# Packed values made in transposed form, and three first halves that share the first layer

## The chip, the cores and the metric

One Trainium2 chip, one core of it. The metric is the device time of one execution in microseconds. Of the kernel before, three runs were timed: 1183.54 us in the median, 1183.08 to 1184.45. TensorE (PE) multiplies, with its weight loads as a row of their own (PEld); VectorE is DVE, ScalarE is ACT, GpSimd is POOL, and SP issues the DMAs.

## The reference

Packed attention followed by two dense layers, all in float32, batch 8, 8 heads, 576 rows, head size 64, 32 packed queries:

```python
p_packed = sm_attn(p, k, v)             # 32 x 64 for each batch and head
out = sm_attn(q, p_packed, p_packed)    # 576 x 64 for each batch and head
x = out.transpose(0, 2, 1, 3).reshape(4608, 512)
h = x @ w_in                            # 512 x 2048
g = where(h > 0, h, exp(min(h, 0)) - 1)
x = g @ w_out                           # 2048 x 512
h = x @ w_in2                           # 512 x 1024
solu = h * softmax(h); ln = layer_norm(solu) * g_ln
out = ln @ w_out2                       # 1024 x 512
```

The weights come as 64-bit floats and are narrowed on the chip.

## The kernel before, in words

The attention of a batch is folded into the first layer. `s1` makes the scores of the packed queries against the keys, for four heads at a time (g = 0, 1): `s1_mm` (line 228), `s1_max`, `s1_exp`, `s1_div`. The probabilities are transposed into `a_sb`, on TensorE for batches 0 and 1 (`t1_mm`, `t1_a`, lines 257 to 263), in 32x32 blocks on VectorE with moves for the later ones (`t1_blocks`, `t1_move`). `pp_mm` (lines 279 to 286) multiplies them with the values: 32 columns of probabilities are the weights, 64 columns of values move, five chunks of rows accumulate, and the four heads lie under each other in PSUM. The trace has two loads and two matmuls for each `pe.matmul` of this type, 40 of each for a run of `pp_mm`. `pp_t` (lines 288 to 295) then turns the result with eight 32x32 transposes on VectorE into `pp_t2`, which has the head's 64 columns in the partitions. `s2_mm` (line 309) makes the scores of half of a batch's 576 rows against the packed keys; `s2_tr` to `s2_split` make their softmax in blocks and split it into two parts, `AT`. `m_mm` (line 353) multiplies the packed values with a quarter c of `w_in`, and `m_a`, `m_b` split the product `M`. So the first layer of a half is `AT` times `M`.

The two layers run in steps. `steps` (lines 722 to 725) lists (batch, half, f), f being one of 16 blocks of 128 of the 2048. A step `n` does `ffn_h` (six matmuls into `h`), the items of the plan, `ffn_g` (lines 385 to 387: two ScalarE instructions and `fe` on VectorE), the split of the step before into `ghi` and `glo` (lines 394 to 396), and `ffn_x2` for the step three before (twelve matmuls with `wo[f // 2]` into `acc`). Batch 0 is done in two rounds: f = 0 to 7 for both halves (steps 0 to 15), then f = 8 to 15 (steps 16 to 31). In the first round the sum is spilled to DRAM (lines 430 to 434); `load_part` brings it back, and line 429 adds it.

Quarters c = 0, 1 of `w_in` and `w_out` blocks 0 to 3 serve the first round, the others the second. One 512-column unit of a 64-bit weight is narrowed by two ScalarE instructions (lines 112, 113), two on VectorE (114, 115) and a product on GpSimd (119); `split_w_out` then splits it on ScalarE and GpSimd.

The order comes from lists written out by hand: `put(n, ...)` attaches an item to step n; `plan_first` holds the steps to 32, `plan_attn(b)` a batch's attention in the 32 steps before its own, `plan_last` the weights of the last layers. The scheduler of the framework orders the instructions by its own model; from step 32 on TensorE alone keeps the program's order (`tc.manual_schedule`, line 739). All loads go through the one queue of SP, in order, and wait there for their buffer: the slots M0 to M4 and wo0 to wo7 hold raw weights, k, v or q before they hold their own tile. The tail (lines 742 to 772) does the two last layers in blocks of 128 rows.

Of the kernel before, what the change touches and what calls it, by code (L numbers as in the profile page):

```python
# [19 lines left out]
NP = 32  # L20
# [14 lines left out]
def attention_mlp_kernel(ctx: ExitStack, tc: tile.TileContext, q, k, v, v_tail, p,  # L35
# [139 lines left out]
    def split_w_out2(j, u):  # L175
        if u == 0:
            wo2[j] = slot(f"wo2_{j}", [P, 2, 1024], f"M{(4 * B + j) % 5}", F32R)
        cs = slice(u * DM, (u + 1) * DM)
        split(wo2[j][:, 0, cs], wo2[j][:, 1, cs], cvs.pop(("wo2", j, u)),
              scale=g_sb[:, 2 * j + u:2 * j + u + 1])  # L180
# [98 lines left out]
    def pp_mm(b, g, ps2=misc_ps):  # L279
        o = ps2(f"pp{b}_{g}")  # L280
        vv = vt.pop((b, g))
        for c in range(5):
            for h in range(4):
                pe.matmul(o[h * NP:(h + 1) * NP, 0, 0:D], a_sb[:, c, h * NP:(h + 1) * NP],
                          vv[:, c, h * D:(h + 1) * D], start=(c == 0), stop=(c == 4))
        st["pp", g] = o

    def pp_t(b, g):

        o = st.pop(("pp", g))  # L290
        for h in range(4):
            for r in range(2):
                n0 = h % 2 * 2 * NP + r * NP
                dve.transpose(pp_t2[b % 2][n0:n0 + NP, 2 * g + h // 2, :],  # L294
                              o[h * NP:(h + 1) * NP, 0, r * NP:(r + 1) * NP])
# [59 lines left out]

    def m_a(b, c):
        mt[b, c] = t = slot(f"M{b}_{c}", [P, 2, 2, 512], f"M{(4 * b + c) % 5}", F32R)
        for g in range(2):
            act.activation(t[:, 0, g], st["m"][:, g], AF.Copy, scale=WSCALE)
        m_lo(t, 0)  # L360
# [201 lines left out]
    def plan_attn(b):  # L562

        n = NSTEP * (b - 1)
        if b == 2:
            n += 2
# [7 lines left out]
        plan_m(b, 0, n + 16 + (b == 2))  # L574
        plan_s2(b, 1, n + 19 + (b == 2), (2, 4, 6, 7, 10, 11))
        plan_m(b, 1, n + 22 + (b == 2))
# [3 lines left out]
    def plan_first():  # L580
# [15 lines left out]
        put(31, (scale_g,))  # L596
# [5 lines left out]
        narrow_w_in(2, 8, 9, 10, 11)  # L602
        narrow_w_in(3, 12, 13, 14, 15)
        for j in range(4, 8):
            narrow_w_out(j, 2 * j + 8, 2 * j + 9)
        put(1, (load_w_in, 3, 0, "M3"))
        put(5, (load_w_out, 5, "M4"))
        put(9, (load_w_in, 3, 1, "wo7"))
        put(11, (load_w_out, 6, "wo6"))
        put(15, (load_w_out, 7, "wo7"))  # L610

        put(0, (s2_mm, 0, 1), (load_q, 1, 0))
        for n, item in ((0, (s2_tr, 0, 1)), (1, (s2_max, 0, 1, pool)), (2, (s2_exp, 0, 1)),
                        (3, (s2_div, 0, 1, pool)), (5, (s2_back, 0, 1)), (6, (s2_split, 0, 1, pool))):
            put(n, item)
        plan_s1(1, 0, 4)
        plan_s1(1, 1, 7)
        put(7, (load_p, 2))
        plan_pp(1, 0, 10)
        m_fast(0, 2, 14)  # L620
        m_fast(0, 3, 16)
        plan_pp(1, 1, 18)
        put(20, (load_part, 0, 0))
        put(27, (load_part, 0, 1))
        plan_s2(1, 0, 22, (1, 2, 4, 5, 7, 8))
        m_fast(1, 0, 24)
        m_fast(1, 1, 26)
        plan_s2(1, 1, 28, (1, 2, 4, 5, 7, 8))
        m_fast(1, 2, 30)
        m_fast(1, 3, 32)  # L630
# [67 lines left out]
    load_w_in(2, 0, "wo7")  # L698
# [5 lines left out]
    load_w_in(2, 1, "wo6")  # L704
# [8 lines left out]
    load_w_out(4, "wo5")  # L713
# [3 lines left out]
    for b in range(2, B):  # L717
# [3 lines left out]

    steps = [(0, half, f, f % 8 == 0, f % 8 == 7)
             for f0 in (0, 8) for half in range(2) for f in range(f0, f0 + 8)]
    steps += [(b, half, f, f == 0, f == NF - 1)
              for b in range(1, B) for half in range(2) for f in range(NF)]
# [10 lines left out]
    for n in range(NSTEP):  # L736
        step(n)

    with tc.manual_schedule(engines={mybir.EngineType.PE}):
        for n in range(NSTEP, len(steps)):  # L740
# [67 lines left out]
```

## Time and profile before

| | |
|---|---|
| median of three runs | 1183.54 us |
| the profiled execution, its own time | 1184.11 us |
| its span | 1182.3 us |
| mean granted clock of TensorE | 0.987 of full speed |
| first `h` matmul | 34.96 us |
| `fe` of step 0 ends | 43.75 us |
| `fe` of step 32 ends | 151.69 us |

The span is the time from the first to the last instruction of the one execution that the profiler recorded. Busy time counts an engine's own instructions. A wait is put down to what came last. Steps are counted by the instructions of line 387, one for each step.

### The profile page before, as it was taken

How to read it: one execution, taken by the hardware profiler on the slowest of the kernel's cores; microseconds unless marked ns; L12 is line 12 of the kernel's file. 1: busy time of each engine (PE TensorE's matmuls, PEld its weight loads, DVE VectorE, ACT ScalarE, POOL GpSimd, SP SyncE). 2: the span in 40 equal slices, each digit the busy share in tenths (PEclk: the TensorE clock that was granted, in tenths of full speed). 3: DMA queues.
4: the chain of work that ended last, by engine and by line, in shares of the span. 5: the costliest groups of instructions: out<-in, count | busy, mean ns of one | idle time of the engine just before them, and what ended most of it. 6: DMA issues, size and time to landing. Idle time of an engine off the chain costs nothing.

```text
span 1182.3 us, 20670 instructions
## 1 busy us (share of the span) xinstructions
PE 1124.3 (95%) x7916; PEld 977.2 (83%) x7916; DVE 854.4 (72%) x1928; ACT 740.5 (63%) x1587; POOL 158.6 (13%) x152
## 2 busy tenths in 40 slices
PE   5688999999999999999999989989999999999997
PEld 1477798898898898898898879978888888888886
DVE  5998876667567567566566595758878878778774
ACT  4788755655655655655655676648766766766664
POOL 2655500100100100100101130200000000000000
PEclk8899999999999999999999999999999999999999
DMA  9763322022022022022011042411111111000001
GB/s 336 295 205 118 96 63 81 21 71 90 4 74 89 3 77 87 2 79 86 1 59 44 2 148 71 143 56 54 31 51 63 34 48 63 27 19 27 28 27 36
DMA packets 39411, 86.01 MB, mean 73 GB/s; under 512 B 7440, under 2 KB 19984, under 8 KB 37392
## 3 DMA queue, kind: packets, MB, share of 16 engines
q1 hardware_dynamic: 39312, 84.69, 21.5%
q8 instruction: 62, 1.02, 0.4%
q14 instruction: 37, 0.30, 0.1%
HBM read 64.62 MB, written 20.05 MB: 72 GB/s over the span
## 4 chain that ended last, share of the span: by engine, by line
PE 46%; DVE 28%; ACT 15%; issue 7%; POOL 2%; DMA 2%; SPq 0%; POOLq 0%; ACTq 0%; DVEq 0%
PE acc L70 9%; PE acc L72 9%; PE acc L71 8%; ACT lnX L501 6%; PE h L70 5%; PE h L71 5%; PE h L72 5%; DVE lnB L491 4%; DVE ln L484 2%; PE m L303 2%; DVE z L476 2%; ACT h L479 2%; DVE a_sb L276 2%; DVE ppT L294 2%; DVE lnT L62 2%
## 5 line engine op out<-in xcount | busy, mean ns | idle before, releaser
L70 PE MATMUL acc<-ghi,wo 128*128 128x288 f32 x1024 | 308.2, 303 | 1.8 <-DVE x L433 1.0
L72 PE MATMUL acc<-glo,wo 128*128 128x288 f32 x1024 | 302.0, 296 | 2.6 <-DVE glo L396 2.5
L71 PE MATMUL acc<-ghi,wo 128*128 128x288 f32 x1024 | 302.5, 296 | 1.3 <-POOL wo L62 1.3
L70 PEld LDWEIGHTS acc<-ghi,wo 128*128 128x128 f32 x1024 | 192.5, 189 | 38.7 <-ACT fe L386 25.8
L72 PEld LDWEIGHTS acc<-glo,wo 128*128 128x128 f32 x1024 | 193.0, 189 | 4.6 <-DVE glo L396 4.6
L71 PEld LDWEIGHTS acc<-ghi,wo 128*128 128x128 f32 x1024 | 193.3, 189 | 2.8 <-POOL wo L62 2.2
L394 ACT CAST ghi<-fe 128x288 fp32r<-128x288 f32 x256 | 110.3, 432 | 132.3 <-DVE fe L387 132.0
L387 DVE SCALAR_TENSOR_TENSOR fe<-fe,h 128x288 f32<-128x288 f32 x256 | 114.9, 450 | 106.8 <-ACT fe L386 105.1
L396 DVE TENSOR_TENSOR glo<-fe,ghi 128x288 fp32r<-128x288 f32 x256 | 135.7, 531 | 76.4 <-ACT ghi L394 75.0
L518 PE MATMUL o<-wo,lnT 128*128 128x512 f32 (+1 forms) x592 | 185.5, 386 | 5.1 <-ACT lnT L61 5.1
L70 PE MATMUL h<-AT,M 128*128 128x288 f32 x512 | 155.5, 304 | 21.9 <-DVE fe L387 16.3
L385 ACT ACTIVATE fe<-h 128x288 f32<-128x288 f32 x256 | 104.4, 408 | 109.2 <-PE h L72 99.2
L501 ACT COPY lnX<-lnB 32x256 f32<-32x256 f32 x288 | 116.3, 404 | 72.8 <-DVE lnB L491 62.1
L71 PE MATMUL h<-AT,M 128*128 128x288 f32 x512 | 152.1, 297 | 0.8 <-DVE M L363 0.8
L72 PE MATMUL h<-AT,M 128*128 128x288 f32 x512 | 151.3, 296 | 0.0
L518 PEld LDWEIGHTS o<-wo,lnT 128*128 128x128 f32 x592 | 111.4, 191 | 27.7 <-ACT lnT L61 5.9
L70 PEld LDWEIGHTS h<-AT,M 128*128 128x128 f32 x512 | 96.6, 189 | 34.8 <-DVE fe L387 25.0
L386 ACT ACTIVATE fe<-fe 128x288 f32<-128x288 f32 x256 | 113.5, 444 | 6.7
L520 PE MATMUL o<-wo,lnT 128*128 128x512 f32 (+1 forms) x296 | 113.6, 385 | 0.0
L71 PE MATMUL h<-wi,x2lo 128*128 128x512 f32 x288 | 112.2, 389 | 1.1 <-DVE x2lo L62 1.1
L70 PE MATMUL h<-wi,x2hi 128*128 128x512 f32 x288 | 112.2, 389 | 0.0
L72 PE MATMUL h<-wi,x2hi 128*128 128x512 f32 x288 | 112.0, 389 | 0.0
(101 smaller groups left out, 1684.9 us busy)
## 6 DMA issues: line engine op xcount, KB each, us to landing
q<-in_q SPq DMA_DIRECT2D x16, 576.0 KB, 4.0
x_dram<-x SPq DMA_DIRECT2D x32, 288.0 KB, 2.3
x2raw<-x_dram SPq DMA_DIRECT2D x9, 1024.0 KB, 5.6
out_x<-y SPq DMA_DIRECT2D x35, 256.0 KB, 2.0
k<-in_k SPq DMA_DIRECT2D x15, 576.0 KB, 4.0
raw_wi<-in_w_in SPq DMA_DIRECT2D x8, 1024.0 KB, 9.4
v_sb<-in_v SPq DMA_DIRECT2D x15, 512.0 KB, 3.9
raw_wo<-in_w_out SPq DMA_DIRECT2D x7, 1024.0 KB, 11.6
```

The source lines that it names most:

```text
L70: pe.matmul(o, a[0], b[0], start=start, stop=False)
L71: pe.matmul(o, a[1], b[0], start=False, stop=False)
L72: pe.matmul(o, a[0], b[1], start=False, stop=stop)
L385: act.activation(e, o[:, 0:HS], AF.Relu, scale=-1.0)
L386: act.activation(e, e, AF.Exp, scale=-1.0)
L387: dve.scalar_tensor_tensor(out=e, in0=e, scalar=-1.0, in1=o[:, 0:HS], op0=ALU.add, op1=ALU.max)
L394: act.copy(ghi, e)
L396: return lambda: dve.tensor_tensor(out=glo, in0=e, in1=ghi.bitcast(F32), op=ALU.subtract)
L491: dve.transpose(t, last.pop(("ln", i)))
L501: act.copy(x, y)
L518: pe.matmul(o, t[:, x, kk], w[:, 0, cs], start=x + kk == 0, stop=x == 1 and kk == 7)
L520: pe.matmul(o, t[:, 0, kk], w[:, 1, cs], start=False, stop=False)
```

## The change

`pp_mm` takes the values as weights (64 columns) and lets the probabilities move (32 columns), so that the product comes out transposed: head 2u + r in partitions 64r to 64r + 63, columns 32u to 32u + 31. `pp_t` is one copy of 128x64. The first round of steps covers three halves, (0, 0), (0, 1) and (1, 0), with f = 0 to 7 each (steps 0 to 23), and the second round the same three with f = 8 to 15 (steps 24 to 47); the half (1, 0) is spilled and reloaded as well. The first plan is written out anew for this: the attention of batch 1 comes earlier, quarters 2 and 3 of `w_in` and blocks 4 to 7 of `w_out` later, and three weight loads leave the preamble. M slots go by a table. The scheduler orders TensorE for the first 64 steps.

```diff
@@ -174,7 +174,7 @@
 
     def split_w_out2(j, u):
         if u == 0:
-            wo2[j] = slot(f"wo2_{j}", [P, 2, 1024], f"M{(4 * B + j) % 5}", F32R)
+            wo2[j] = slot(f"wo2_{j}", [P, 2, 1024], m_slot(B, j), F32R)
         cs = slice(u * DM, (u + 1) * DM)
         split(wo2[j][:, 0, cs], wo2[j][:, 1, cs], cvs.pop(("wo2", j, u)),
               scale=g_sb[:, 2 * j + u:2 * j + u + 1])
@@ -277,22 +277,21 @@
                                 t[h * NP:(h + 1) * NP, j::4])
 
     def pp_mm(b, g, ps2=misc_ps):
+
+
         o = ps2(f"pp{b}_{g}")
         vv = vt.pop((b, g))
-        for c in range(5):
-            for h in range(4):
-                pe.matmul(o[h * NP:(h + 1) * NP, 0, 0:D], a_sb[:, c, h * NP:(h + 1) * NP],
-                          vv[:, c, h * D:(h + 1) * D], start=(c == 0), stop=(c == 4))
+        for u in range(2):
+            for c in range(5):
+                for r in range(2):
+                    h = 2 * u + r
+                    pe.matmul(o[r * D:(r + 1) * D, 0, u * NP:(u + 1) * NP], vv[:, c, h * D:(h + 1) * D],
+                              a_sb[:, c, h * NP:(h + 1) * NP], start=(c == 0), stop=(c == 4))
         st["pp", g] = o
 
     def pp_t(b, g):
-
-        o = st.pop(("pp", g))
-        for h in range(4):
-            for r in range(2):
-                n0 = h % 2 * 2 * NP + r * NP
-                dve.transpose(pp_t2[b % 2][n0:n0 + NP, 2 * g + h // 2, :],
-                              o[h * NP:(h + 1) * NP, 0, r * NP:(r + 1) * NP])
+        dve.tensor_copy(pp_t2[b % 2][:, 2 * g:2 * g + 2].rearrange("p u n -> p (u n)"),
+                        st.pop(("pp", g))[:, 0, 0:2 * NP])
 
     def packed_mm(o, b, x):
 
@@ -353,8 +352,14 @@
         packed_mm(o, b, wi[c])
         st["m"] = o
 
+    def m_slot(b, c):
+
+        k = 4 * (b - 2) + c
+        first = {(0, 0): 0, (0, 1): 1, (1, 0): 2, (1, 1): 3, (0, 2): 4, (0, 3): 0, (1, 2): 1, (1, 3): 4}
+        return f"M{first[b, c] if b < 2 else (0, 2, 3, 1, 4)[k % 5]}"
+
     def m_a(b, c):
-        mt[b, c] = t = slot(f"M{b}_{c}", [P, 2, 2, 512], f"M{(4 * b + c) % 5}", F32R)
+        mt[b, c] = t = slot(f"M{b}_{c}", [P, 2, 2, 512], m_slot(b, c), F32R)
         for g in range(2):
             act.activation(t[:, 0, g], st["m"][:, g], AF.Copy, scale=WSCALE)
         m_lo(t, 0)
@@ -562,8 +567,6 @@
     def plan_attn(b):
 
         n = NSTEP * (b - 1)
-        if b == 2:
-            n += 2
         plan_s1(b, 0, n)
         plan_s1(b, 1, n + 3)
         put(n + 3, (load_p, b + 1))
@@ -571,9 +574,9 @@
         plan_pp(b, 1, n + 10)
         plan_s2(b, 0, n + 14, (1, 2, 4, 6, 8, 9))
         n = NSTEP * (b - 1)
-        plan_m(b, 0, n + 16 + (b == 2))
-        plan_s2(b, 1, n + 19 + (b == 2), (2, 4, 6, 7, 10, 11))
-        plan_m(b, 1, n + 22 + (b == 2))
+        plan_m(b, 0, n + 16)
+        plan_s2(b, 1, n + 19, (2, 4, 6, 7, 10, 11))
+        plan_m(b, 1, n + 22)
         plan_m(b, 2, n + 25)
         plan_m(b, 3, n + 28)
 
@@ -593,41 +596,47 @@
             put(n1, (split_w_out, j, 0, pool))
             put(n1 + 1, (split_w_out, j, 1, pool))
 
-        put(31, (scale_g,))
+        put(40, (scale_g,))
         put(0, (split_w_out, 0, 0, pool), (split_w_out, 0, 1, dve))
         narrow_w_in(1, 0, 0, 1, 1)
         m_fast(0, 1, 2)
         for j in range(1, 4):
             narrow_w_out(j, 2 * j, 2 * j + 1)
-        narrow_w_in(2, 8, 9, 10, 11)
-        narrow_w_in(3, 12, 13, 14, 15)
-        for j in range(4, 8):
-            narrow_w_out(j, 2 * j + 8, 2 * j + 9)
-        put(1, (load_w_in, 3, 0, "M3"))
-        put(5, (load_w_out, 5, "M4"))
-        put(9, (load_w_in, 3, 1, "wo7"))
-        put(11, (load_w_out, 6, "wo6"))
-        put(15, (load_w_out, 7, "wo7"))
+        put(1, (load_w_in, 2, 0, "wo7"))
+        put(3, (load_w_in, 2, 1, "wo6"))
+        put(6, (load_w_out, 4, "wo5"))
+        put(8, (load_w_out, 5))
+        narrow_w_in(2, 10, 12, 14, 16)
+        put(13, (load_w_in, 3, 0, "wo7"))
+        put(17, (load_w_in, 3, 1, "wo6"))
+        narrow_w_out(4, 17, 18)
+        narrow_w_in(3, 19, 20, 21, 23)
+        put(16, (load_w_out, 6, "M1"))
+        put(21, (load_w_out, 7, "wo7"))
+        narrow_w_out(5, 24, 25)
+        narrow_w_out(6, 28, 29)
+        narrow_w_out(7, 30, 31)
 
         put(0, (s2_mm, 0, 1), (load_q, 1, 0))
-        for n, item in ((0, (s2_tr, 0, 1)), (1, (s2_max, 0, 1, pool)), (2, (s2_exp, 0, 1)),
-                        (3, (s2_div, 0, 1, pool)), (5, (s2_back, 0, 1)), (6, (s2_split, 0, 1, pool))):
+        for n, item in ((0, (s2_tr, 0, 1)), (0, (s2_max, 0, 1, pool)), (1, (s2_exp, 0, 1)),
+                        (1, (s2_div, 0, 1, pool)), (2, (s2_back, 0, 1)), (3, (s2_split, 0, 1, pool))):
             put(n, item)
-        plan_s1(1, 0, 4)
-        plan_s1(1, 1, 7)
-        put(7, (load_p, 2))
-        plan_pp(1, 0, 10)
-        m_fast(0, 2, 14)
-        m_fast(0, 3, 16)
-        plan_pp(1, 1, 18)
-        put(20, (load_part, 0, 0))
-        put(27, (load_part, 0, 1))
-        plan_s2(1, 0, 22, (1, 2, 4, 5, 7, 8))
-        m_fast(1, 0, 24)
-        m_fast(1, 1, 26)
-        plan_s2(1, 1, 28, (1, 2, 4, 5, 7, 8))
-        m_fast(1, 2, 30)
-        m_fast(1, 3, 32)
+        plan_s1(1, 0, 0)
+        plan_s1(1, 1, 2)
+        put(3, (load_p, 2))
+        plan_pp(1, 0, 4)
+        plan_pp(1, 1, 6)
+        plan_s2(1, 0, 9, (1, 2, 3, 4, 5, 6))
+        m_fast(1, 0, 14)
+        m_fast(1, 1, 18)
+        m_fast(0, 2, 22)
+        put(28, (load_part, 0, 0))
+        m_fast(0, 3, 25)
+        put(35, (load_part, 0, 1))
+        plan_s2(1, 1, 27, (1, 2, 3, 4, 5, 6))
+        m_fast(1, 2, 36)
+        m_fast(1, 3, 38)
+        put(43, (load_part, 1, 0))
 
     def plan_last():
 
@@ -695,13 +704,11 @@
     load_p(1)
     load_k(1, 0)
     load_v(1, 0)
-    load_w_in(2, 0, "wo7")
     s2_mm(0, 0)
     s2_tr(0, 0)
     cv_w_in(0, 3)
     s2_max(0, 0, dve)
     s2_exp(0, 0)
-    load_w_in(2, 1, "wo6")
     s2_div(0, 0, dve)
     m_mm(0, 0)
     s2_back(0, 0)
@@ -710,7 +717,6 @@
     m_b(0, 0)
     cv_w_out(0, 0)
     cv_w_out(0, 1)
-    load_w_out(4, "wo5")
     sp.dma_start(out=g_sb, in_=g_ln)
 
     plan_first()
@@ -718,11 +724,9 @@
         plan_attn(b)
     plan_last()
 
-
-    steps = [(0, half, f, f % 8 == 0, f % 8 == 7)
-             for f0 in (0, 8) for half in range(2) for f in range(f0, f0 + 8)]
-    steps += [(b, half, f, f == 0, f == NF - 1)
-              for b in range(1, B) for half in range(2) for f in range(NF)]
+    steps = [(i // 2, i % 2, f, f % 8 == 0, f % 8 == 7)
+             for f0 in (0, 8) for i in range(3) for f in range(f0, f0 + 8)]
+    steps += [(i // 2, i % 2, f, f == 0, f == NF - 1) for i in range(3, 2 * B) for f in range(NF)]
     def step(n):
         ffn_h(*steps[n])
         rest = ffn_split(*steps[n - 1]) if n > 0 else lambda: None
@@ -733,11 +737,12 @@
         if n >= LAG:
             ffn_x2(*steps[n - LAG])
 
-    for n in range(NSTEP):
+    FREE = 2 * NSTEP
+    for n in range(FREE):
         step(n)
 
     with tc.manual_schedule(engines={mybir.EngineType.PE}):
-        for n in range(NSTEP, len(steps)):
+        for n in range(FREE, len(steps)):
             step(n)
     ffn_split(*steps[-1])()
     ctx.enter_context(tc.manual_schedule(engines={mybir.EngineType.PE}))
```

## Rows read from the trace of the kernel before

**Rows 1.** The page of the profile: busy time by engine, and VectorE in 40 slices.

```profile
PE 1124.3 (95%) x7916; PEld 977.2 (83%) x7916; DVE 854.4 (72%) x1928; ACT 740.5 (63%) x1587; POOL 158.6 (13%) x152
...
DVE  5998876667567567566566595758878878778774
```

**Rows 2.** Busy time in stretches; columns: length, PE, PEld, DVE, ACT, POOL, PEclk, DMA, GB/s.

```profile
35.00:43.80 8.80, 6.15 (x36) 3.42 (x36) 8.66 (x15) 6.54 (x14) 4.17 (x4) 0.74 1.04 368
43.80:101.80 58.00, 50.15 (x390) 41.70 (x390) 54.29 (x96) 47.11 (x101) 34.26 (x28) 1.00 0.51 180
101.80:128.80 27.00, 25.18 (x214) 19.51 (x215) 24.01 (x47) 21.27 (x48) 16.77 (x14) 0.94 0.30 90
128.80:151.75 22.95, 21.93 (x185) 18.77 (x186) 16.81 (x33) 15.69 (x37) 9.43 (x8) 1.00 0.39 124
151.75:195.50 43.75, 43.18 (x396) 40.03 (x396) 31.92 (x97) 22.54 (x55) 0.00 (x0) 1.00 0.23 71
...
240.45:328.95 88.50, 87.88 (x770) 80.09 (x770) 57.12 (x149) 49.62 (x115) 7.47 (x6) 1.00 0.18 55
```

**Rows 3.** Stretches again, line 387 alone; columns: length, DVE busy (count), PEclk, DMA.

```profile
43.80:101.80 58.00, 7.05 (x16) 1.00 0.51 180
```

**Rows 4.** VectorE's groups by shape between 35 and 151.75 us: the weight narrowing.

```profile
L115 DVE SCALAR_TENSOR_TENSOR cv_wo<-raw_wo,cv_wo 128x512 uint32<-128x512 uint32 x16 | 14.9, 933 | 0.2
...
L115 DVE SCALAR_TENSOR_TENSOR cv_wi<-raw_wi,cv_wi 128x512 uint32<-128x512 uint32 x12 | 11.6, 965 | 0.3
L114 DVE TENSOR_SCALAR cv_wo<-cv_wo 128x512 uint32<-128x512 uint32 x16 | 10.5, 659 | 2.1 <-ACT cv_wo L112 2.0
```

**Rows 5.** What TensorE waited for between 240 and 600 us: total, times, longest.

```profile
PE h L70 <- DVE fe L387: 1.7, 4, 0.4
PE s L303 <- DVE ppT L294: 0.8, 4, 0.2
```

**Rows 6.** Timeline of the lead-in: start, length, engine, line, operation.

```profile
20.18 1.19 PE L303 MATMUL s<-q,ppT 64*32 64x288 f32 x8
...
22.50 0.42 DVE L294 STREAM_TRANSPOSE ppT<-pp 32x32 f32<-32x32 f32 x2
...
22.97 3.31 PE L303 MATMUL s<-q,ppT 64*32 64x288 f32 x8 [1.61 <-DVE ppT L294]
...
23.67 1.39 DVE L294 STREAM_TRANSPOSE ppT<-pp 32x32 f32<-32x32 f32 x6
...
26.32 0.85 DVE L320 STREAM_TRANSPOSE u<-s 128x288 f32<-128x288 f32 x2
```

**Rows 7.** Timeline of VectorE in the first 32 steps.

```profile
79.29 0.27 DVE L263 COPY a_sb<-t 64x128 f32<-64x128 f32 x1
...
85.63 1.79 DVE L294 STREAM_TRANSPOSE ppT<-pp 32x32 f32<-32x32 f32 x8
...
136.88 0.74 DVE L429 SCALAR_TENSOR_TENSOR part<-acc,part 128x576 f32<-128x576 f32 x1
...
140.72 1.29 DVE L363 SCALAR_TENSOR_TENSOR M<-m,M 128x512 fp32r<-128x512 f32 x2 [0.37 <-ACT M L359]
...
145.90 0.78 DVE L344 STREAM_TRANSPOSE a<-u 128x576 f32<-128x576 f32 x1 [1.03 <-POOL u L340]
```

**Rows 8.** What SP's DMA queue waited for, up to 240 us.

```profile
SPq L97 <- DVE cv_wo L115: 36.4, 5, 20.1
SPq L202 <- PE s L228: 26.4, 4, 12.8
```

**Rows 9.** Timeline of TensorE in a steady batch: one `m`.

```profile
299.87 1.09 PE L303 MATMUL m<-wi,ppT 64*32 64x512 f32 x16
```

**Rows 10.** A steady packed-value run; weight loads of 32 and 64 columns, ns min/median/max.

```profile
263.22 0.60 PEld L284 LDWEIGHTS pp<-v_sb,a_sb 128*32 128x32 f32 x40 [0.17 <-issue]
263.22 0.77 PE L284 MATMUL pp<-v_sb,a_sb 128*32 128x64 f32 x40
...
L284 PEld LDWEIGHTS pp<-v_sb,a_sb x600: 106/110/110, 13.9 to 628.8; 128*32 128x32 f32 x150
...
L228 PEld LDWEIGHTS s<-k,pt_bd x128: 132/137/231, 5.2 to 601.9; 128*64 128x64 f32 x128
```

## The prediction

> **What bounds the kernel now.** The page comes first: TensorE is busy for 95% of the span, and VectorE is fullest in the second to fifth slice [rows 1]. A share over the whole span mixes stages, so the second view cuts the span at steps, a step being one f of `steps`, told by its `fe` instruction of line 387. In a steady batch of 32 steps TensorE is busy 87.88 of 88.50 us, 2.77 us a step, with VectorE at 57.12 [rows 2]: TensorE sets the pace, and only TensorE work or a TensorE wait counts there. In the first steps it is the other way: the first 16 after 43.8 us took 58 us, 3.6 us a step [rows 2, 3], VectorE busy 54.29 of it (94%); in the next eight it is 89%, in the eight after those 73% at 2.87 us a step, close to the pace of TensorE. What fills VectorE there is the narrowing of the 64-bit weights: 12 and 16 units at lines 114 and 115, some 1.6 us a unit [rows 4]. So the kernel has a VectorE-bound start of 24 steps and a TensorE-bound rest up to the tail. In the steady part the wait list for TensorE holds 2.5 us in four batches, all of it for VectorE: 0.62 us a batch [rows 5].
>
> The profiled execution took 1184.1 us, its span 1182.3; the median of the runs is 0.6 lower. I sum against 1184.1.
>
> **The lead-in.** The eight 32x32 transposes of `pp_t(0, 1)` run from 22.50 to 25.06 us with a weight instruction between; the second half of the score matmuls waits for them piece by piece, and `u` starts at 26.32 [rows 6]. The one copy of 64 columns that takes their place is not in the trace; the nearest row is a PSUM copy of 128 columns at 0.27 us [rows 7], so I take 0.27 (at least nothing; at most 0.42, the two transposes at 22.50). From 22.8 the eight matmuls need the 1.19 us that the first eight took [rows 6], and `u` starts at 24.0: **-2.3 us**. If the scheduler puts the copy behind another narrowing, half of that is left.
>
> **The first 32 steps, VectorE's account.** Its work between 35 and 151.75 us was 8.66 + 54.29 + 24.01 + 16.81 = 103.8 us [rows 2]. All narrowing still has to be over by step 32, so sharing a half over three halves removes none of it; it moves it. What leaves this stretch:
> - `pp_t(1, .)`: two runs of eight transposes at 1.79 us become two copies at 0.27: -3.0 [rows 7].
> - `m(1, 2)` moves from step 31 to step 37: -1.3. The transpose back of `s2(1, 1)` falls at step 32: -0.8. The two final evictions of half (0, 0) move from step 26 to 34, and one first eviction of (1, 0) is new, on VectorE: -1.5 + 0.7 [rows 7].
>
> That leaves 97.9 us. VectorE was busy 94% and 89% of the two stretches that it bounds; I take 91% for all 32 steps, since the weights are now spread over all of them: 97.9 / 0.91 = 107.6 us, from 35 - 2.3 to 140.3. Before it was 151.75: **-11.5 us**, lead-in included. TensorE's own floor lies below: 43.8 - 2.3 + 88.5 + 1.1 for one more `m` = 131. So VectorE stays the bound, but with 9 us between the two. Bounds: 96% gives 134.7 (-17), 85% gives 147.9 (-4).
>
> Moved steps and their queues: the score, softmax and value steps of batch 1 now lie in steps 0 to 15 beside thirteen narrowing units instead of eighteen. Their GpSimd parts (subtract, multiply, split) queue behind narrowing products in order, and VectorE's `s2_div` and `s2_back` wait for them, with `fe` and `glo` of the FFN queued behind. Work is conserved; the wait costs only what lowers the 91%. On SP's queue the three weight loads that stood in the preamble go to steps 1, 3 and 6. Loads waited there for the narrowing to free their buffer, 36.4 us in all, and the k loads 26.4 us for the score matmuls [rows 8]; with fewer blocking loads ahead, k, v and q of batch 1 are issued sooner. I cost SP at nothing: its cover is that each load has several steps before its use. If that cover is gone, a step waits for a whole landing. The extra spill of half (1, 0) (two stores and two loads of 288 KB on SP's queue among the k and p loads of batch 2) falls where the kernel moves 71 GB/s [rows 2]; nothing.
>
> **Steps 32 to 48.** TensorE-bound, 43.18 busy of 43.75 [rows 2]. `m(1, 2)` comes here: 16 matmuls, 1.09 us [rows 9]: **+1.1 us**. The final evictions are covered by VectorE's 12 idle us. Up to step 63 TensorE's order is now the scheduler's and no longer the program's. Steps 24 to 31, in the scheduler's order, took 0.1 us a step more than a steady batch, so 32 steps may cost 0 to 3 us; I take nothing, as VectorE's 73% in those steps explains the difference. The new M slots and the later `scale_g` cost nothing: each slot's last reader lies at least one step before its next writer.
>
> **The packed values on TensorE, batches 2 to 7.** Before: 40 weight loads of 32 columns and 40 matmuls of 64 columns in 0.60 and 0.77 us [rows 10]; less the length of the last one, 39 starts in 0.55, 14 ns apart. That is four column tiles side by side, each taking 55 ns for a step. After: 64 columns of weights, 32 columns moving, two tiles side by side. How 64-column loads pace a run of such short matmuls no row shows. A load of 32 columns takes 110 ns and one of 64 takes 137 [rows 10]: 27 ns for 32 more columns, so 54 for a load of 64, against half the streaming of before. Lower bound: loads stay hidden, the same 14 ns, nothing. Middle: each tile is now bound by its loads, 54 ns for two tiles, 27 ns apart: 40 x 27 = 1.08 us, 0.52 more. Upper: loads one after the other, 40 x 54 = 2.16, 1.6 more. I take the middle, as the row shows loads of separate tiles overlapping (40 of 27 ns in series would be 1.08, and the row has 0.60). Twelve runs lie in the TensorE-bound part: **+6.2 us** (0 to 19). Those of batches 0 and 1 lie beside the VectorE bound.
>
> The Trainium skill, "TensorE: Matmul & The Clock Gate", section "LDWEIGHTS (loading the stationary operand)", has the load's time grow with its columns, P / 1.2 ns. The difference between the two rows agrees; taken as a series it would be 2.13 us a run and 19 us in the sum, which the narrow run of this trace does not bear out.
>
> **VectorE relief in the steady part.** 1.5 us less per run of `pp_t`. The 0.62 us that TensorE waits in a batch [rows 5] is VectorE's lateness around the values' transposes and moves; I let it go whole: 6 x 0.62 = **-3.7 us** (0 at worst; what is late next is the following `fe`, which then has more than a microsecond to spare). The tail after 690 us has no attention and is untouched.
>
> **Sum**: -11.5 + 1.1 + 6.2 - 3.7 = -7.9 us: 1176.2 on the profiled execution, 1175.6 on the median. I say 1176.
>
> **Rivals.**
> *A: TensorE's floor is reached.* If work spread evenly lets VectorE keep 96% or above and GpSimd's product interferes less with it, step 32 falls near 131 to 135. For it: VectorE shows 98% in the 8.8 us before 43.8 [rows 2]. Against: 89% as soon as the work mixes with batch 1's chain. Sum: -19 + 3.6 = -15: 1168; with hidden loads 6 less, 1162.
>
> *B: slower, by the loads.* The place is the twelve runs of packed values in the TensorE-bound batches; the price is the 64-column load. Break-even where 12x = 11.5 - 1.1 + 3.7, x = 1.2 us a run more than now, a run of about 2 us. At the upper bound, 1.6 us, the sum is -11.5 + 1.1 + 19.2 - 3.7 = +5: 1189. For it: TensorE has no slack there, so it is paid in full. Against: the overlap of the narrow loads. The Trainium skill's page named above would give about this time if its loads did not overlap.
>
> *C: the start gains little.* Batch 1's chain, packed into 16 steps at one link a step, makes VectorE wait for GpSimd and TensorE for batch 1's first half at step 16. At 86% of VectorE step 32 falls at 32.7 + 113.8 = 146.5, the gain is 5 us, and the 3.6 us of the rest take most of it: 1182. At 84% it is slower by 1. For it: 89% in the stretch where that chain stood beside narrowing. Against: the chain has fewer units beside it now.
>
> **How the numbers follow.** A measurement of this kernel can tell about 0.2%, 2.4 us, from no change. Forecast 0.48, all of it faster. A 0.14, faster. B 0.10, slower. C 0.28: 0.06 faster, 0.13 within, 0.09 slower. So faster 0.68, same 0.13, slower 0.19. The range runs from 1165, between A's two figures, to 1185, C with 84%; it leaves out most of B and the end of A. The likeliest case alone, with VectorE at 89 to 94% and loads at 0 to 0.7 us, is 1168 to 1181.
>
> **What would show it.** Right: the 32nd step near 140 us and VectorE above 88% of the stretch to there; one copy of 128x64 in place of each eight transposes, under 0.3 us; the packed-value run of 40 matmuls at about 1.3 us where it was 0.77; a steady batch near 88.9 us with no wait for `fe` left. Wrong: a step 32 below 134 (A) or above 146 (C); a run of 2 us or more and batches above 91 us (B); a run that stays at 0.77, which puts the batch at 87.9 and takes 6 us off the sum; and TensorE waiting at step 16 for the first `AT` of batch 1, which no term holds.

## The result, and the profile after

The changed kernel takes 1198.57 us (median of four runs, 1198.12 to 1200.13) where four runs of the kernel before give 1183.31 us (1181.57 to 1184.45): a ratio of 1.0125, interval 1.0110 to 1.0139. It is **slower**, by 15 us, and the forecast of 1176 was wrong in sign. The profiled execution took 1198.6 us, its span 1196.8, at a mean granted clock of 0.99.

Where the time went is read from the ends of the steps, one `fe` for each (line 387 before, 392 after). The last six columns are experiments of the next section (E2 is experiment 2, and so on).

| step ends, us | before | after | E2 | E3 | E13 | E14 | E15 | E16 |
|---|---|---|---|---|---|---|---|---|
| 0 | 43.8 | 44.7 | 44.2 | 38.0 | 43.1 | 44.1 | 43.7 | 38.5 |
| 4 | 59.8 | 68.3 | 59.8 | 62.4 | 59.2 | 69.4 | 58.3 | 54.8 |
| 8 | 69.4 | 83.1 | 70.2 | 78.1 | 70.3 | 81.2 | 74.1 | 64.8 |
| 12 | 81.7 | 98.0 | 81.1 | 89.9 | 81.1 | 91.4 | 89.0 | 76.0 |
| 16 | 101.7 | 116.3 | 110.9 | 101.7 | 96.2 | 105.6 | 105.1 | 94.1 |
| 24 | 128.7 | 137.9 | 138.9 | 125.3 | 116.9 | 127.7 | 131.7 | 115.6 |
| 32 | 151.7 | 157.8 | 157.8 | 151.7 | 141.3 | 150.7 | 155.5 | 139.9 |
| 64 | 240.4 | 252.9 | 253.6 | 244.9 | 230.1 | 246.2 | 244.8 | 228.9 |
| 224 | 683.6 | 697.4 | 698.1 | 689.6 | 673.3 | 690.7 | 689.3 | 672.1 |

After against before: 14.6 us lost by step 16, 8.5 won back by step 32, 6.5 lost in steps 32 to 63, and 0.25 in each steady batch. The stretches of [rows 2] again, with the same cuts in time (so other steps fall in them), and a last row that ends with step 32:

```profile
43.80:101.80 58.00, 49.42 (x390) 41.20 (x391) 52.36 (x91) 43.87 (x93) 35.93 (x28) 0.91 0.47 163
...
128.80:151.75 22.95, 22.59 (x166) 20.76 (x166) 16.63 (x40) 14.57 (x36) 4.66 (x4) 1.00 0.55 178
...
240.45:328.95 88.50, 88.50 (x763) 81.07 (x762) 53.64 (x133) 49.54 (x114) 7.46 (x6) 1.00 0.18 55
...
35.00:157.75 122.75, 106.03 (x822) 90.55 (x814) 104.34 (x187) 90.14 (x196) 65.86 (x51) 0.94 0.46 159
```

In the first 58 us the instruction counts of TensorE are as before, yet the granted clock is 0.91 where it was 1.00. VectorE is busy 85% up to step 32 (104.34 of 122.75), and its work has not shrunk: before it was 103.8 us. In the steady batch TensorE has no idle time left.

Cut at the steps, from the end of step 0 to the end of step 16, TensorE is idle 11.3 us of 71.66 where it was idle 7.8 of 57.97: 3.5 us more. The 96 matmuls of `h` in these steps, as many as before, take 4.0 us more (first before, then after; the columns are length, PE busy, clock, DMA, GB/s), and the 192 of `acc` take 31.68 us where they took 29.35:

```profile
43.75:101.72 57.97, 16.20 (x96) 1.00 0.51 181
```

```profile
44.67:116.33 71.66, 20.17 (x96) 0.90 0.47 161
```

The same work at a lower granted clock is thus 6.3 of the 13.7 us that these steps take longer, the largest part. Some 4.4 us are other TensorE work that now lies here, batch 1's scores, transposes and packed values above all; later steps have less of it, which is part of what they win back.

What TensorE waited for between 35 and 120 us (total, times, longest):

```profile
PE h L70 <- DVE fe L392: 8.1, 5, 3.5
...
PE h L70 <- ACT M L364: 2.1, 1, 2.1
PE m L302 <- ACT e L241: 1.7, 1, 1.7
```

The first is spread over steps 0 to 16: its longest, 3.5 us, comes at 44.7 us (1.8 before), with narrowing ahead of `fe` on VectorE. The second and third belong together. All small products share one PSUM buffer (`misc_ps` has a single one). The timeline of TensorE shows that the scheduler gave it first to the packed scores of batch 1 (`s`), and `m` of batch 0's second quarter had to wait until ScalarE had read them in `e`:

```profile
49.37 1.19 PE L228 MATMUL s<-k,pt_bd 128*64 128x288 f32 x8
...
55.00 1.09 PE L302 MATMUL m<-wi,ppT 64*32 64x512 f32 x16 [1.69 <-ACT e L241]
...
61.27 0.85 PE L70 MATMUL h<-AT,M 128*128 128x288 f32 x2 [2.07 <-ACT M L364]
62.48 0.61 PE L71 MATMUL h<-AT,M 128*128 128x288 f32 x1 [0.37 <-DVE M L368]
62.88 0.44 PE L72 MATMUL h<-AT,M 128*128 128x288 f32 x1
```

Before, that `m` ran between 40.5 and 48 us. The `h` of step 4 needs it, and when that `h` starts at 61 us TensorE has just been idle and takes 0.24 us from one to the next, twice the 0.13 us it takes at full clock. The chain of waits in the same stretch shows the way from `m` to `h`:

```profile
57.03 0.42 DVE cv_wo L114
...
57.48 0.70 DVE cv_wo L115
...
58.31 1.22 POOL cv_wo L119
59.56 0.62 ACT wo L61
60.18 0.56 ACT cm_wo L113
60.73 0.98 ACT M L364 x2
61.73 0.70 DVE M L368
```

`M` is late because ScalarE's copy of it (line 364) stands in ScalarE's queue behind the split of `wo` (line 61), which waits for GpSimd's product (119), which waits for VectorE's narrowing (114, 115). One unit of narrowing crosses three queues, and whatever stands behind it in any of them waits for the other two. (This is read from the trace; no run takes that hand-over away by itself.)

In steps 32 to 63, now ordered by the scheduler, TensorE has no wait at all, and still takes 95.2 us where it took 88.7. Its timeline shows why: five of the six `m` are cut, four in two pieces and one in three, and one run of scores in two, with work of the steps between the pieces. The first and the one that stayed whole:

```profile
160.10 1.04 PE L302 MATMUL m<-wi,ppT 64*32 64x512 f32 x2
...
162.06 1.08 PE L302 MATMUL m<-wi,ppT 64*32 64x512 f32 x14
...
203.30 1.09 PE L302 MATMUL m<-wi,ppT 64*32 64x512 f32 x16
```

Two of these matmuls take nearly as long as sixteen, which run side by side in the array [rows 9].

### The profile page after: what moved, and what is told of

It reads as the page before. It is cut to its first block, busy times and chain, and to the rows that moved or that the text cites. A ratio compares the mean times of both kernels' runs of the same rounds, so it can differ in the third digit from the quotient of the medians.

```text
span 1196.8 us, 20590 instructions
## 1 busy us (share of the span) xinstructions
PE 1140.3 (95%) x7916; PEld 994.3 (83%) x7916; DVE 837.5 (70%) x1818; ACT 740.5 (62%) x1587; POOL 160.7 (13%) x152
## 4 chain that ended last, share of the span: by engine, by line
PE 53%; DVE 22%; ACT 13%; issue 6%; DMA 4%; POOL 1%; SPq 0%; POOLq 0%; ACTq 0%; DVEq 0%
PE acc L70 11%; PE acc L72 10%; PE acc L71 10%; ACT lnX L506 6%; PE h L70 5%; PE h L71 5%; PE h L72 5%; DVE lnB L496 4%; PE m L302 3%; DVE ln L489 2%; DVE z L481 2%; ACT h L484 2%; DVE glo L401 2%; DVE lnT L62 2%; DVE x2lo L62 2%
## 5 line engine op out<-in xcount | busy, mean ns | idle before, releaser
L401 DVE TENSOR_TENSOR glo<-fe,ghi 128x288 fp32r<-128x288 f32 x256 | 141.0, 553 | 74.6 <-ACT ghi L399 72.5
L70 PE MATMUL h<-AT,M 128*128 128x288 f32 x512 | 157.4, 308 | 21.1 <-DVE fe L392 17.9
L506 ACT COPY lnX<-lnB 32x256 f32<-32x256 f32 x288 | 116.3, 404 | 72.5 <-DVE lnB L496 62.1
L72 PE MATMUL h<-AT,M 128*128 128x288 f32 x512 | 153.0, 299 | 1.4 <-DVE AT L62 1.4
L71 PE MATMUL h<-AT,M 128*128 128x288 f32 x512 | 153.6, 300 | 0.4 <-DVE M L368 0.4
```

What stands on the lines that cost most here:

```text
L70: pe.matmul(o, a[0], b[0], start=start, stop=False)
L71: pe.matmul(o, a[1], b[0], start=False, stop=False)
L72: pe.matmul(o, a[0], b[1], start=False, stop=stop)
L401: return lambda: dve.tensor_tensor(out=glo, in0=e, in1=ghi.bitcast(F32), op=ALU.subtract)
L506: act.copy(x, y)
```

## The experiments

Each time stands beside runs of the kernel before on the same chip (medians 1183.4 for experiments 1 to 4, 1183.2 for 5 to 8, 1184.1 for 9 to 12; one run of 1183.2 for 13 to 16; 9, 10 and 13 to 16 are single runs). Every edit changes the scheduler's order as a whole, so a difference of a few us at one step is not the edit's alone.

### 1: TensorE in program order from step 32

```diff
-    FREE = 2 * NSTEP
+    FREE = NSTEP
```

> The changed kernel with TensorE's program order kept from step 32 on, as before, and not from step 64. Theory of the cut runs: in steps 32 to 63 the scheduler cut small packed runs (five of the m products, a score run, two value runs) in two, and each cut m costs 1.0 us; whole runs give 5.5 to 6.5 us back, steps 32 to 64 take 89.5 us where they took 95.2, and the time is about 1192.5. Rival, the stretch is longer by the work moved into it (one m more, wider loads, evictions): steps 32 to 64 stay at 94 or more and the time within 2 us of 1198.6. Steps 0 to 32 are the same under both.

1192.85 us, ratio 1.0082 (1.0067 to 1.0097): 5.7 below the changed kernel. Line 302 alone over steps 32 to 63, first the changed kernel, then this one; columns: length, PE busy, PEld busy, clock, DMA:

```profile
157.75:252.92 95.17, 14.84 (x128) 2.34 (x128) 1.00 0.18 57
```

```profile
156.15:247.28 91.13, 7.97 (x128) 1.48 (x128) 1.00 0.23 71
```

The same 128 matmuls take 6.9 us less, for seven cuts. The stretch shortens by 4.0 only: the fixed order brings back waits of 1.6 us, 1.2 of them for `M`, and a run of batch 2's scores (1.19 us) that the scheduler had done ahead of step 32 now lies in it. Without it step 32 ends 1.6 us earlier, which makes up the 5.7. The cost of the cut runs is shown.

### 2 and 11: batch 1's chain two steps later

```diff
-        plan_s1(1, 0, 0)
-        plan_s1(1, 1, 2)
-        put(3, (load_p, 2))
-        plan_pp(1, 0, 4)
-        plan_pp(1, 1, 6)
-        plan_s2(1, 0, 9, (1, 2, 3, 4, 5, 6))
+        plan_s1(1, 0, 2)
+        plan_s1(1, 1, 4)
+        put(5, (load_p, 2))
+        plan_pp(1, 0, 6)
+        plan_pp(1, 1, 8)
+        plan_s2(1, 0, 11, (1, 2, 3, 3, 4, 4))
```

> The changed kernel with batch 1's score and value chain two steps later, so that m(0, 1) comes before the first score run of batch 1 on TensorE and in the one small PSUM buffer. Theory of the PSUM order: step 4 needs m(0, 1), which waited behind s1(1, 0) in that buffer until 55 us; with m first, step 4 is back at about 60 us (68.3 in the changed kernel), the clock does not fall, step 16 is at 103 to 107 (116.3), and the time is 1186 to 1191. Rival, narrowing pulled forward: VectorE still does 18 to 20 narrowing units before step 16, so step 16 stays above 112 and the time above 1194.

1199.15 us, ratio 1.0135. The table shows the theory right up to step 12, which ends at 81.1 us, no later than before; so the 16 us lost there in the changed kernel come from the place of the chain. The total gains nothing, against 1186 to 1191 expected: steps 13 to 16 take 29.8 us (before 20.0). What TensorE waited for between 81 and 111 us:

```profile
PE h L72 <- POOL AT L62: 2.3, 1, 2.3
PE acc L72 <- DVE glo L401: 2.1, 1, 2.1
PE h L70 <- ACT AT L61: 1.1, 1, 1.1
```

The first half of batch 1 begins at step 16, and its `AT` is now late. GpSimd's timeline shows a narrowing product ahead of its half of `AT`:

```profile
104.08 1.21 POOL L119 TENSOR_TENSOR wi<-cv_wi,cm_wi 128x512 f32<-128x512 f32 x1 [1.93 <-ACT AT L61]
105.26 1.85 POOL L62 TENSOR_TENSOR AT<-a,AT 128x576 fp32r<-128x576 f32 x1
```

Experiment 11 joins this edit with that of experiment 1.

> The changed kernel with batch 1's chain two steps later and TensorE in program order from step 32 on. If the two act on different stretches, steps 32 to 64 take 90 to 91.5 and the start is that of the run with the chain later (step 32 at 156 to 159): 1192 to 1195. Rival, whole runs also let the work that is left over from the start catch up: under 1190.

1194.18 us, ratio 1.0085 (1.0061 to 1.0109): experiment 1 helps here as it did there, the later chain again gives nothing.

### 3 and 6: VectorE in program order

```diff
     FREE = 2 * NSTEP
-    for n in range(FREE):
-        step(n)
+    with tc.manual_schedule(engines={mybir.EngineType.DVE}):
+        for n in range(FREE):
+            step(n)
```

> The changed kernel with VectorE's program order kept for the first 64 steps, so that the narrowing stays at the steps where the plan has it (13 to 15 units before step 16 and not 20). Theory of the narrowing pulled forward: step 16 at 103 to 107 and the time 1187 to 1192. Theory of the PSUM order: m(0, 1) is still behind s1(1, 0), step 4 stays above 65 us, and what the calmer steps 4 to 16 give back is under 4 us: 1194 or more. In either case an order by hand can make VectorE wait for ScalarE or GpSimd where the scheduler had other work; that would show as waits in VectorE's list of over 10 us up to step 16.

1190.98 us, ratio 1.0064 (1.0047 to 1.0081), the fastest version that keeps the changed steps and all their work. Step 32 ends where it did before, by another road. All that it gains on the changed kernel by then is there at the end of step 0 (38.0 us against 44.7), ahead of which six units of narrowing lie in place of ten; from there to step 32 it takes 113.7 us, the changed kernel 113.1. Stretches of 20 us (columns as in rows 2):

```profile
60.00:80.00 20.00, 17.89 (x179) 16.95 (x179) 14.87 (x30) 15.58 (x35) 12.04 (x10) 0.91 0.34 104
...
140.00:160.00 20.00, 17.60 (x110) 14.78 (x110) 19.39 (x29) 13.96 (x31) 15.12 (x12) 0.91 0.23 69
```

In the first, no engine is full, VectorE at 74%; in the last, VectorE is at 97%, with the narrowing that was left over. The scheduler had pulled narrowing forward: 20 units lie in steps 1 to 16 of the changed kernel (17 before), where the plan has 13 to 15. Program order keeps the plan, and the plan is no better.

Experiment 6 takes VectorE's order for 32 steps and TensorE's from there on.

```diff
+    with tc.manual_schedule(engines={mybir.EngineType.DVE}):
+        for n in range(NSTEP):
+            step(n)
     with tc.manual_schedule(engines={mybir.EngineType.PE}):
-        for n in range(FREE, len(steps)):
+        for n in range(NSTEP, len(steps)):
```

> The changed kernel with VectorE in program order for the first 32 steps and TensorE in program order from step 32 on: the two repairs so far together. If they add, the start is that of the run with VectorE in order (step 32 at 150 to 153 us) and steps 32 to 64 take 90 to 91.5, and the time is 1187 to 1190. If VectorE's order of steps 32 to 63 mattered as well, it is off by more than 2 us.

1196.97 us, ratio 1.0117: a miss. Step 32 ends at 151.0, but steps 32 to 63 then take 101.2 us: TensorE, which may not reorder, waits there 3.7 us for the two parts of `wo`, narrowed late, and 2.8 for `e` to clear the one PSUM buffer.

### 4 and 5: each part alone

Experiment 4 is the kernel before with the new `pp_mm` and `pp_t` and nothing else; experiment 5 is the changed kernel with the old two.

> The kernel before with the transposed packed values alone. A run of 40 matmuls takes 1.36 us as in the changed kernel where it took 0.77; a steady batch goes from 88.5 to 88.7 to 88.8 us, since 0.6 of the 1.2 us is VectorE lateness given back. If that and nothing in the lead-in is all, 1.5 us are lost in six batches and up to 3 us gained in the first 32 steps: 1181 to 1185. Rival, the wide loads are the loss of the change: plus 5 us or more, 1188 or above. Rival, the lead-in gets its 2.3 us and the first steps 3 more: 1179 or below.

> The changed kernel with the old packed values (four heads under each other, eight transposes): the new step list and plan alone. If the loss is in the order of the start, step 16 stays at 112 to 118 us and steps 32 to 64 at 93 to 96; the steady batches go back to 88.5, and the time is 1194 to 1199. Rival, the transposed form makes the loss in the start (its shorter VectorE work lets the scheduler pull narrowing forward): step 16 at 105 or less and the time 1188 or less.

1190.03 us, ratio 1.0056 (1.0041 to 1.0071), and 1204.80 us, ratio 1.0179 (1.0162 to 1.0196). Both missed their forecasts (1181 to 1185, 1194 to 1199). The time of experiment 4 is the one that its rival gave, the wide loads as the loss, but not for that reason: it gains 1.3 us by step 16, has lost 1.9 by step 32 and 3.1 by step 64, and adds 0.25 a batch from there, and 1.3 us behind step 224. In experiment 5 the steady batch is back at 88.5 us, and steps 32 to 63 take 98.3, with still more cut `m`. With the changed kernel the four corners are 1183.3, 1190.0, 1204.8 and 1198.6: the new packed values cost 6.7 with the old steps and save 6.2 with the new ones. The parts don't add, since each changes what the scheduler does with the start.

### 7 and 8: a plan written anew

Experiment 7 is experiment 6 with the chain two steps later, the late narrowing spread over steps 9 to 29 and `s2` of batch 1's second half at step 30; in experiment 8 TensorE keeps program order from step 0 too. Its core:

```diff
-        narrow_w_in(2, 10, 12, 14, 16)
+        narrow_w_in(2, 9, 10, 12, 14)
...
-        narrow_w_out(7, 30, 31)
+        narrow_w_out(7, 28, 29)
```

> The same with batch 1's chain two steps later (m(0, 1) ahead of it in the PSUM buffer) and the second weights' narrowing planned some two steps earlier, evenly over steps 9 to 29. If the start is VectorE's work in an order that either starves the FFN or piles up late, an even order gives step 32 at 140 to 147 and the time 1178 to 1184: sharing three halves then gains up to what the prediction had. Rival, VectorE in a fixed order waits too long for ScalarE and GpSimd whatever the order: step 32 at 150 or more, the time 1187 or more.

> The run before with TensorE's program order from step 0 on, so that no m run is cut in the start (three cut ones there, 1 us for each cut, some 4 us). Theory of the cut runs in the start: step 32 earlier by 2 to 4 us than in the run before. Rival, the cuts fill TensorE's idle time there, and a fixed order makes it wait behind late operands: step 32 later by 2 us or more.

1198.87 us (ratio 1.0132) and 1197.70 us (1.0116). Step 32 ends at 159.1 and 159.0: both miss, and the even plan reaches step 32 no sooner than the scheduler's order did (157.8).

### 9, 10 and 16: less narrowing in the kernel before

Line 114 gone (9), line 113 gone and GpSimd multiplying by a constant (10), both (16).

```diff
-        act.activation(m, high, AF.Sign)
-        dve.tensor_scalar(out=t, in0=t, scalar1=3, scalar2=None, op0=ALU.logical_shift_left)
...
-        nc.gpsimd.tensor_tensor(out=dst, in0=t, in1=m, op=ALU.mult)
+        nc.gpsimd.tensor_tensor(out=dst, in0=t, in1=ones.to_broadcast([P, n]), op=ALU.mult)
```

> The kernel before without VectorE's shift of line 114 in every narrowing unit (the weights come out wrong in scale; the instruction count and all else stay). Some 19 us of VectorE's work between 35 us and step 32 are gone. If VectorE alone bounds the start, as the prediction's account has it, step 32 comes at 131 to 137 us, at TensorE's floor, where it was at 151.7. Rival, the start is bound by a chain through ScalarE, VectorE and GpSimd in turn, each in order: step 32 at 142 to 148, and the next run gives about as much.

> The kernel before without ScalarE's sign of line 113 in every narrowing unit (GpSimd multiplies with a constant, so the weights lose their sign). Some 18 us of ScalarE's work between 35 us and step 32 are gone. If VectorE alone bounds the start: step 32 within 3 us of 151.7. If ScalarE is in the chain that bounds it: step 32 at 142 to 148.

> The kernel before without the two instructions of lines 113 and 114 in every unit, each of which alone gave 2 us at step 32. If the start hangs on a chain through both engines, the two together give more than the sum, step 32 at 140 to 146; if it hangs on neither, step 32 stays at 146 to 150.

1179.08, 1171.66 and 1165.76 us; part of that is the last narrowing, after step 224, so the start is read from step 32. It ends at 150.0, 149.5 and 139.9: 1.7, 2.2 and **11.8** us earlier. Of this 1.5, 0.9 and 5.2 us are there at the end of step 0, and 0.1, 1.3 and 6.5 come from there to step 32. Experiment 9 fell in neither of its ranges; 10 came within 3 us of 151.7, as if VectorE alone set the start, which 9 rules out; 16 is where a chain through both engines was to put it, at the edge. The stretch from 43.8 to 101.8 us of each, in this order:

```profile
43.80:101.80 58.00, 51.28 (x392) 43.39 (x389) 46.18 (x80) 49.15 (x108) 38.38 (x31) 0.97 0.50 181
```

```profile
43.80:101.80 58.00, 51.27 (x394) 42.24 (x393) 50.44 (x100) 38.40 (x85) 34.22 (x29) 1.00 0.52 189
```

```profile
43.80:101.80 58.00, 51.79 (x429) 44.32 (x431) 47.98 (x86) 44.61 (x98) 43.72 (x36) 1.00 0.58 202
```

Without line 114 VectorE falls from 54.29 us of this stretch [rows 2] to 46.18, and TensorE does two matmuls more. Without line 113 ScalarE falls from 47.11 to 38.40, and it does four more. Without both it does 39 more, and GpSimd gets 36 pieces of work where it had 28. Neither engine's work alone sets the start; that of both together does. No engine is busy over 90% in any of the three, so no full engine is the bound there, which speaks for a chain through both; which of its links it is, these runs don't show.

### 12: the kernel before in program order from step 24

```diff
-    for n in range(NSTEP):
+    for n in range(24):
         step(n)
...
-        for n in range(NSTEP, len(steps)):
+        for n in range(24, len(steps)):
```

> The kernel before with TensorE in program order from step 24 on in place of 32. If cut runs cost TensorE time wherever it is the bound, steps 24 to 32 (22.95 us before) take 21.5 to 22.5 and the time is 0.5 to 1.5 us lower, 1182 to 1182.8, which would beat both kernels. Rival, VectorE and ScalarE still set the pace there and a fixed order waits for them: 0 to 3 us slower.

1188.32 us, ratio 1.0034 (1.0022 to 1.0047), 4.2 us slower where even the rival allowed 3. TensorE's waits between 125 and 160 us:

```profile
PE acc L70 <- ACT wo L61: 3.1, 1, 3.1
PE acc L71 <- POOL wo L62: 2.0, 1, 2.0
```

In that part of the kernel the fixed order waits for the narrowing, where the scheduler went round it. Program order on TensorE pays here only once the narrowing is over.

### 13, 14 and 15: the narrowing or the chain left out

Experiments 13 (kernel before) and 14 (changed kernel) don't load, narrow or split quarters 2 and 3 of `w_in` and blocks 4 to 7 of `w_out`, and use the first ones in their place; 15 is the changed kernel without batch 1's packed scores, transposes and packed values. The skipped items:

```diff
+            if fn in (load_w_in, cv_w_in) and args[0] > 1 or fn in (load_w_out, cv_w_out, split_w_out) and args[0] > 3:
+                continue
```

```diff
+            if fn in (s1_mm, s1_max, s1_exp, s1_div, t1_mm, t1_a, pp_mm, pp_t) and args[0] == 1:
+                continue
```

> The kernel before without loading, narrowing and splitting quarters 2 and 3 of w_in and blocks 4 to 7 of w_out; the first ones are used in their place (16 of the narrowing units gone, some 25 us of VectorE, 21 us of ScalarE and 31 us of GpSimd). This is the most that any later placing of the second weights could give. If narrowing bounds the start in any way, step 32 comes at 132 to 138 us; if the start is bound by the FFN's own chain and batch 1's, at 143 or later, and sharing a half over three had little to win.

> The same omission in the changed kernel. Theory of the narrowing pulled forward: nothing is left to pull forward, step 16 comes at 98 to 105 us where it came at 116.3. Theory of batch 1's chain: step 4 still above 64 and step 16 at 110 or later, since m(0, 1) still waits in the PSUM buffer behind s1(1, 0).

> The changed kernel without batch 1's packed scores, softmax, transposes and packed values (its packed values are zero; the scores of the second attention and the m products stay). Theory of batch 1's chain: step 4 at 56 to 60 us, step 16 at 98 to 104. Theory of the narrowing pulled forward: VectorE takes still more units in its place, step 16 at 110 or later.

1169.91, 1186.54 and 1189.66 us. Experiment 13 sets the ceiling of the idea, as the scheduler orders it: with the second set of weights wholly gone, the old steps reach step 32 at 141.3 us, 10.4 earlier, between the two ranges expected. The new steps with the same relief (14) reach it at 150.7, so they lose the ceiling again, all of it by step 8 (81.2 against 70.3). Stretches of 20 us, 13 and then 14:

```profile
60.00:80.00 20.00, 17.62 (x158) 14.50 (x157) 18.71 (x39) 16.46 (x38) 10.87 (x9) 1.00 0.49 147
80.00:100.00 20.00, 20.00 (x143) 17.00 (x143) 7.24 (x16) 9.41 (x22) 0.00 (x0) 1.00 0.17 52
```

```profile
60.00:80.00 20.00, 14.26 (x111) 12.51 (x111) 12.85 (x25) 13.78 (x31) 10.51 (x9) 0.83 0.46 141
80.00:100.00 20.00, 20.00 (x199) 18.16 (x198) 11.62 (x26) 11.83 (x27) 2.33 (x2) 1.00 0.35 117
```

From 80 us on TensorE is full in both. Ahead of it, in 14, no engine is: TensorE idles and its granted clock falls to 0.83. The waits of 14 between 43 and 106 us name two places met above:

```profile
PE h L70 <- DVE fe L392: 8.1, 2, 4.6
PE m L302 <- ACT e L241: 1.7, 1, 1.7
```

The longer wait for `fe`, 4.6 us up to 69.4, ends the same relay: on ScalarE the first instruction of `fe` stands behind a split of `wo` that waits for GpSimd's product.

```profile
67.62 0.62 ACT L61 CAST wo<-cv_wo 128x512 fp32r<-128x512 f32 x1 [0.94 <-POOL cv_wo L119]
68.14 0.40 ACT L390 ACTIVATE fe<-h 128x288 f32<-128x288 f32 x1
```

Without the chain (15) step 4 ends at 58.3 us, and the loss comes later. It is not narrowing pulled forward, of which 16 units lie in steps 1 to 16, one less than before; VectorE is busy 95% in steps 5 to 8 and over 99% in steps 9 to 12, and why is open. Step 16 comes about 1 us behind the range that the narrowing (14: 98 to 105) or the chain (15: 98 to 104) was to give, and step 4 of 14 is late, as the chain's theory had it. At step 16 either omission takes about 11 us off the 116.3: the chain and the narrowing each cost that much in the presence of the other.

## Why the prediction was wrong, point by point

**The first 32 steps, VectorE's account: the step that failed.** It set work over a busy share, 97.9 us at 91%, and got step 32 at 140.3. Measured: 104.34 us at 85%, and 157.8. (Before, the share over all these steps was 89%, 103.8 of 116.75 us; the 91% came from two of the three stages.) The share is a symptom. Experiments 9, 10 and 16 show that one instruction of each narrowing unit (18.6 us in all for line 114) can leave VectorE, or one ScalarE, with hardly an effect, while both together give 11.8 us. I read this with the chain above: the start hangs on a relay through the queues of three engines. The lower clock that followed its waits, 6.3 us in 16 steps, is in no term. The work was wrong as well. VectorE's groups over 35 us to step 32, as in rows 4, with the idle time ahead:

```profile
L401 DVE TENSOR_TENSOR glo<-fe,ghi 128x288 fp32r<-128x288 f32 x32 | 24.3, 774 | 4.4 <-ACT ghi L399 4.1
L392 DVE SCALAR_TENSOR_TENSOR fe<-fe,h 128x288 f32<-128x288 f32 x33 | 14.4, 447 | 7.6 <-ACT fe L391 7.4
...
L234 DVE TENSOR_REDUCE nm<-s 128x1 f32<-128x576 f32 x4 | 3.0, 750 | 0.4 <-PE s L228 0.4
```

`glo` got slower by its mean alone (774 ns against 669 before), and four `nm` instead of two show that the scheduler brought batch 2's scores in. `fe` waited 7.4 us for ScalarE (2.9 before).

The account also had the direction of the trade wrong. I counted that the weights may come later; that is worth at most 10.4 us in the scheduler's order (13). What it takes is batch 1's chain in the first 16 steps, which I costed at "what lowers the 91%". The runs put its price at 9 to 13 us by the end of step 8 (83.1 us with the chain in its place, 70.2 and 74.1 in experiments 2 and 15). By the traces it is paid in the one PSUM buffer, which the prediction never looked at (1.7 us for `m`, then 2.5 for `M`), in the relay and in the lower clock that follows; no run tells these apart. The prediction did name the queues of GpSimd and VectorE, and left out ScalarE's, where `M` stood.

The Trainium skill, "Perfetto Trace Analysis", section "Identifying the Most-Contended Engine", advises to find the engine with the highest occupancy and optimize it first. In this start that would be VectorE at 94%; the runs differ, since 8 us less of it (9) moved step 32 by 1.7 us.

**The lead-in** gave nothing: `u` starts at 26.30 us (26.32 before). The packed values of this stage take 2.69 us (18.59 to 21.28; before they ended at 20.25), which the sum left out. The copy takes 0.21 us, as foreseen, but comes at 23.66, behind two narrowing pieces:

```profile
21.76 0.42 DVE L114 TENSOR_SCALAR cv_wi<-cv_wi 128x512 uint32<-128x512 uint32 x1
22.21 1.52 DVE L115 SCALAR_TENSOR_TENSOR cv_wi<-raw_wi,cv_wi 128x512 uint32<-128x512 uint32 x1
23.66 0.21 DVE L293 COPY ppT<-pp 128x64 f32<-128x64 f32 x1
```

"Half of that is left", I wrote for that case; the narrowing pieces behind it took the other half ahead of `u`.

**Steps 32 to 63 in the scheduler's order.** Two `m` came to these steps and not one, as the scheduler had run `m(1, 3)` at 149.25 us before: line 303 had 96 matmuls there, line 302 has 128, and the term of +1.1 should have been +2.2. For the order I took nothing, bound 0 to 3 us; it is about 5.7 (1). The bound came from steps 24 to 31 of before, in which the two `m` happen to be whole. One that is cut in three stands a few steps ahead in the same trace, and I didn't read it:

```profile
116.87 1.04 PE L303 MATMUL m<-wi,ppT 64*32 64x512 f32 x2
...
118.83 1.06 PE L303 MATMUL m<-wi,ppT 64*32 64x512 f32 x8
...
120.28 1.06 PE L303 MATMUL m<-wi,ppT 64*32 64x512 f32 x6
```

**The packed values** were nearly right: +0.52 us a run forecast, +0.59 measured, between the ends as argued:

```profile
74.80 1.36 PE L288 MATMUL pp<-a_sb,v_sb 128*64 128x32 f32 x40
```

By the Trainium skill, "TensorE: Matmul & The Clock Gate", section "LDWEIGHTS (loading the stationary operand)", 40 loads of 64 columns one after the other would take 2.13 us, an estimate from its P / 1.2 ns. The trace does not bear that sum out: the whole run takes 1.36 us. **VectorE's relief** was right: nothing is left of the waits of [rows 5], and the batch grows by 0.25 us where 1.18 of longer runs were added, so 0.9 came back (0.62 forecast; the other 0.3 I can't place).

**The rivals.** B named the right sign for the wrong cause: its loads cost 0.25 us a batch net. C had the place and part of the mechanism, batch 1's chain packed into 16 steps with VectorE waiting (for ScalarE, though, not for GpSimd), and its price, 1182, was far too small. "TensorE waiting at step 16 for the first `AT`", listed as what no term holds, is what experiment 2 met.

**Open.** Which of the relay's hand-overs sets the start was not isolated: each edit moves the scheduler's order. A second PSUM buffer for `m` was not tried, nor was the kernel before with VectorE in program order ahead of step 0, an order by which that step ended 6.7 us earlier in experiment 3 than in the changed kernel. No version that does all the work ran faster than the kernel before.

## What to carry to other kernels

Where several engines hand work on in a fixed queue order, an engine's busy share alone is no bound: take work off each engine alone, and off both, before an account is built on one. When a chain is moved earlier, look for the single buffer that it passes through and for what stood there. And where TensorE is the bound, keep packed runs of small matmuls whole: fix their order there, and leave the order free where late weights are still arriving.

## What was not expected of the hardware

A run of sixteen `m` matmuls that work side by side takes 1.09 us, two of them take 1.04, and each cut of a run costs about 1.0 us (6.9 us for seven, experiment 1). One copy of 128x64 out of PSUM takes 0.21 us where eight 32x32 transposes of the same values took 1.79 [rows 7]. After the idle stretches of the start TensorE works at its lower level, 1.2 GHz, `h` matmuls 0.24 us apart instead of 0.13, so that a wait there is paid for a second time: the granted clock was 0.74 in the mean from 60 to 80 us:

```profile
60.00:80.00 20.00, 17.47 (x123) 14.54 (x124) 15.19 (x29) 15.99 (x35) 12.07 (x10) 0.74 0.46 146
```
